# A fused RWKV-6 and GELU kernel: the last blocks' burst moved into the kv burst, the chunks' products in one burst by bank parity, and new slots

## The chip, the cores and the metric

The kernel runs on one core of a Trainium2 chip. The metric is the time of one execution in device microseconds (us). Before the change three runs gave 581.32, 579.07 and 582.42 us, a median of 581.32. Engines are named PE (TensorE), DVE (VectorE), ACT (ScalarE), POOL (GpSimd) and SP (SyncE, which issues most DMAs here).

## The reference

An RWKV-6 recurrence over 4 x 8 heads, 768 steps and a head size of 48, and behind it, token by token, a two-layer network with an exact GELU (384 to 2048 to 384, 3072 tokens), all in fp32:

```python
for t in range(S):
    cur = np.einsum('bhd,bhe->bhde', u[None] * kt, vt)
    y[:, :, t] = np.einsum('bhd,bhde->bhe', rt, state + cur)
    state = wt[:, :, :, None] * state + np.einsum('bhd,bhe->bhde', kt, vt)
x = y.transpose(0, 2, 1, 3).reshape(B * S, H * D)
h = x @ w_in
g = 0.5 * h * (1.0 + erf(h / sqrt(2)))
out = g @ w_out
```

## The kernel before

The tokens are cut into eight pieces of 384. For each piece `attention(x, unit)` makes the recurrence's output and leaves it, transposed, in `xT`; `mlp(x)` (for the first piece `first_mlp`) turns `xT` into 384 rows of the result. Both are Python generators, and the strings in `PLAN`, one for each stage, say in which order their steps are emitted: in stage x "." is a step of the network for piece x-1 on PE, "s" the second part of the recurrence for piece x, "f" the first part of the one for piece x+1, "v", "g", "o" and "e" the network's merges, GELUs, sums and copies (DVE, ACT, POOL), "l" loads, "x" and "w" sums of blocks of x and of the weights. The order of emission is the order of each engine's queue. Nothing else schedules: an engine takes its instructions in that order and waits on semaphores where data or a buffer is not ready. From stage 2 on the network's products follow a scheme of fewer multiplications with block sums (lists `PRODUCTS`, `OUT_PRODUCTS`), so that a stage holds 160 big matmuls (128x128 weights, 192 columns); an fp32 matmul shows as two records in the trace. Between them stand bursts of small 64x64 matmuls, which use the four quarters of the array.

The recurrence works in chunks of 64 steps. Inside a chunk it needs a lower triangle of products of r and k, scaled by running products of w, in `a_sb` (`at`). For pieces 2 to 7 `quarters()` builds it on two levels (`h` = 4 and 16). On each level twelve blocks (`n_b`) go through PE in three bursts (`cuts = (0, 5, 10, n_b)`: five, five and two blocks; 40, 40 and 16 records), each into a pair of PSUM banks of its own from `pair("d")`. From stage 2 on there are two such pairs, shared with `kv_ps` and `y_ps`. `copy_quarters` moves a burst's blocks into `at`: on the first level DVE with masks (L737), on the last ACT in six copies (`copy_rows`, L724). Between the bursts and the copies DVE scales r and k for the next level; on the last level k is then transposed in 32x32 blocks (L657), moved by 12 DMAs (L652) and four ACT copies (L806) to k transposed.

Then come, with `yield` between them:

- the burst `kv_ps` (L822): k transposed times v for each chunk, 96 records in two pairs of banks;
- `chain_states` (L837, L842): 20 small updates on DVE that carry the state from chunk to chunk, reading `kv_ps`;
- `inside()` (L863): the chunks' own products, `at` times v, 96 records into two pairs `y_ps`. For p = 0 and 1 the lower and the upper 64 rows of the array write to the pair's first and second bank;
- `fences()` (L873, L875): DVE copies two columns of `y_ps` to a tile that nobody reads, so that the states' products wait until the own products of both row halves are written;
- the products of r with the states (L908), 80 or 96 records, added into `y_ps`;
- the copies of `y_ps` to `xT` on ACT (L934, L931) and by DMA (L938).

Of the network, L1040 is `multiply`, L1084 and L1082 are ACT's copies out of PSUM, L1133 the GELU, L1115, L1117 and L1120 merges, L1161, L1164 and L1167 the sums for the output, L1036 and L1034 the sums of x. L512 and L499 begin the next piece's recurrence on DVE.

Of the kernel before, what the change touches and what calls it, by code (L numbers as in the profile page):

```python
# [38 lines left out]
PLAN = {  # L39
    0: "l.s....llsl.lssslslss.lc.l.slslls...ssss..lcs.s.s.l.ss..ss..sccs.c.s.llpssslw..cs.ffpccxx",  # L40
    1: (
        "l.ccswccclss.cw.l.ccccccscs.c.csscccc.scc.sscwccc.cswcs.wcsccscccls.c.ssc.sclcswcwcc.wcwcc"
        "sslcw..cwlclwccswclsc.cf.w.cw..ccc.cfw..cfyx....f.x..x.f.yxxf.wxw..y..y...wywyx..xyxf.yw.f"
        ".wxywxyl.yf."
    ),
    2: (
        "s.w..s.w.w.s..w..wswv.w..v.ww.vwv.ssw.swgww.swgsvwv.w.sgwv.wssls..wvsw...wg...g...wvsw.gvl"
        "s..sgvss...gg.ssvgvw.wvgvgvv.glsgv..gs.og.l.oe.s.wsoeo.s...seooe..l.so.ooe.lewo...o..ooeoe"
        "..os.eolol.s.se..oo.oew.lsw.ooosles..f.fo.oo.o.fo..xooxxfxxxxxfxfxx"
    ),  # L50
    3: (
        ".ls....v..s.sl...g...s.vvs..s..l.vg.gvg....s..l..sv.svss.ssss.g.svssgvlvg.sg..vv.vv.gsv.gv"
        "s.sggv.gslsvs..g.ogsog.e..s.eoo.....seo.oe.os.eoo.e...oooso.e.e.s.soo.ool.lessseo..oeolssf"
        "....fooo.e..f.xooxo.o..x.oooxlxxxfxfxfxx"
    ),
    4: (
        "ls.....s.ss.v....g....vlv.s.gs.vv..g....sv...s.glssvvgsvslsss..gvs.v.gs.ggss..v.sgv.vv..vv"
        ".slsggs.svsg.gog.g.s.oss.eo.e.o..o.so..ee..ooo..eoe.o..oosee.s..loo.os.oes.e.so.llsleo.of."
        "s.o.esolo.f..f.ooo.o.foo..xoxxxxxxxffxfxx"
    ),  # L60
    5: (
        ".....sll....v....vv..vsg.vs....ggs.v..vs.ls..g.sv.ssssvs.sl..g.vs.vsvgs.s.ggv.gss..l..vsvv"
        "vsssvg...ggsggogsg.os.oe.se.l.o..o..o.oe.es.o.oeeo....o..ooseoes..ose.loos.ssell..oo.eossf"
        "..o..fo.oeof..o..xoo.oxox.oxxlxxxffxfxx"
    ),
    6: (
        "s..sl...v.....v..g..ss.v.lvv...g.gvs..gsv..s.v..s.ssggsssvss..ss.l.vg.s..vg.vvggss..vvvv.."
        "ssssvggg..g.so.ggsoe...seo...ssols.o.o.eooe...o.e.eo.o.o.e.ooeo..ssl.oos.lsel..eslooo..lef"
        "s..oes.o.lfo..foo.o.o..fooxoxxxxxffxxxfxx"
    ),  # L70
    7: (
        "....sv.......gss.v....vsv..g..sg..vvg..s...s.svsgvsvss.ss.ss.vvgs.v.gsg.vg..svg...vv.ssgsv"
        "v.gg.g.sgso.gseo..es.....osso..ooo.eeoo..e.eso...oooee...os.soe..oos.se.s.oeosos...oo.e..."
        "oooo..oxo.oxx.oxxxxxxxx"
    ),
    8: (
        "..........v...v...v.v..g.gggv.v.....vv.....g.gvg....vgv.vvvgvgv..vgg..g.vgo..gge..eo...o.o"
        ".oo.eoe....oeo.e.o..o.oeeo..oo.eo.o.eo....ooe..o.e.oo.o..o.oo.oo.o"
    ),
}  # L80

# [111 lines left out]
def kernel(  # L193
# [31 lines left out]
    def pair(name):  # L225
        return pools["d"].tile([128, 2, BANK], F32, name=name, tag="d")
# [250 lines left out]
    def attention(x, unit):  # L477
# [183 lines left out]
        def quarters():  # L661
# [28 lines left out]
            for h in QUARTERS:  # L690
                m, r4, t4, s0, s1, s2 = views(h)

                def burst(first, behind):

                    d = pair("d")
                    if behind == n_b and h == FINE:
                        for a in range(FINE):
                            for g in range(2):
                                for p in range(2):
                                    nc.tensor.matmul(fine_of(d, g)[half[p], a * n_b:],  # L700
                                                     lhsT=places[half[g], a, p * C:(p + 1) * C],
                                                     rhs=fine_sb[half[g], 0:FINE - a, a],
                                                     start=(a == 0), stop=True, skip_group_check=True)
                    for n in range(first, behind):
                        i = n - first
                        for g in range(2):
                            for p in range(2):
                                nc.tensor.matmul(d[half[p], g, i * 3 * C // 2:(i + 1) * 3 * C // 2],  # L708
                                                 lhsT=kc[half[g], n // NI, n % NI, p],
                                                 rhs=rx[half[g], 2 * n + p], start=True, stop=True,  # L710
                                                 skip_group_check=True)
                    return d
# [99 lines left out]
        def vs(b, i, g):  # L812
            o = ((parts[b] * NI + i) * 2 + g) * D
            return loaded[x][1][:, o:o + G]

        kvs = []
        for b in range(np_):
            kv_ps = pair("kv_ps")
            for i in range(NI):
                for p in range(2):  # L820
                    for g in range(2):
                        nc.tensor.matmul(kv_ps[half[g], p, i * D:(i + 1) * D], lhsT=k_t(b, i, p, g),  # L822
                                         rhs=vs(b, i, g)[half[p], 0:D], start=True, stop=True)
# [21 lines left out]
        def swap(b):  # L845
            return parts[b] % 2
# [20 lines left out]
        def fences():  # L867

            for y, y_ps in ys:
                fence = wk.tile([128, 2], F32, name="fence")  # L870
                if split:
                    for c in range(2):
                        nc.vector.tensor_copy(out=fence[:, c:c + 1], in_=y[c][:, NI * C - 1:NI * C])  # L873
                else:
                    nc.vector.tensor_copy(out=fence, in_=y_ps[:, :, NI * C - 1])  # L875

        if x == 0:

# [18 lines left out]

        for i in range(NI):
            for p in range(2):
                for b in range(np_):  # L900
                    q, c3 = divmod(i, N3)
                    for g in range(2):
                        c = 2 * c3 + (p + g) % 2
                        src, c0 = (st, c - 1) if c else (before, NC - 1)
                        if src is None:
                            continue
                        o = ((parts[b] * Q + q) * NC + c0) * D
                        nc.tensor.matmul(ys[b][0][c % 2][half[g ^ swap(b)], i * C:(i + 1) * C],  # L908
                                         lhsT=src[half[g], o:o + G], rhs=rc[half[g], b, i, c % 2],
                                         start=False, stop=True, skip_group_check=True)  # L910
# [415 lines left out]
```

## Time and profile before

| what | value |
|---|---|
| runs, median (lowest to highest) | 581.32 us (579.07 to 582.42) |
| the profiled execution's own time | 584.98 us |
| its span from first to last instruction | 583.20 us |
| PE busy | 557.0 us, 96%, clock granted 1.0 |
| DVE busy | 491.9 us, 84% |
| ACT busy | 330.3 us, 57% |
| POOL busy | 103.1 us, 18% |
| DMA | 62.15 MB, mean 107 GB/s |

By stage (start and end in us, then busy us):

| stage | from | to | PE | DVE | ACT |
|---|---|---|---|---|---|
| 0 | 0 | 45.3 | 35.3 | 36.2 | 18.8 |
| 1 | 45.3 | 125.4 | 78.2 | 73.9 | 54.2 |
| 2 | 125.4 | 190.8 | 64.3 | 59.6 | 39.2 |
| 3 | 190.8 | 257.5 | 65.7 | 60.3 | 38.7 |
| 4 | 257.5 | 326.0 | 66.8 | 61.9 | 38.8 |
| 5 | 326.0 | 393.4 | 65.3 | 59.4 | 38.6 |
| 6 | 393.4 | 460.1 | 64.9 | 60.1 | 38.7 |
| 7 | 460.1 | 528.6 | 65.3 | 54.7 | 38.7 |
| 8 | 528.6 | 583.2 | 51.1 | 25.9 | 24.7 |

A timeline line has the start, the length, the engine, the line of the kernel, the operation, out<-in, the shape, how many were merged, and in brackets the idle time of the engine before it with what ended it. "issue" there means that the engine waited for nothing that the profile shows. A group's line ends with busy time, mean time of one, and idle time before them.

### The profile page before, as it was taken

How to read it: one execution, taken by the hardware profiler on the slowest of the kernel's cores; microseconds unless marked ns; L12 is line 12 of the kernel's file. 1: busy time of each engine (PE TensorE's matmuls, PEld its weight loads, DVE VectorE, ACT ScalarE, POOL GpSimd, SP SyncE). 2: the span in 40 equal slices, each digit the busy share in tenths (PEclk: the TensorE clock that was granted, in tenths of full speed). 3: DMA queues.
4: the chain of work that ended last, by engine and by line, in shares of the span. 5: the costliest groups of instructions: out<-in, count | busy, mean ns of one | idle time of the engine just before them, and what ended most of it. 6: DMA issues, size and time to landing. Idle time of an engine off the chain costs nothing. (4 is left out here: it accounts for less than half of the span.)

```text
span 583.2 us, 17698 instructions
## 1 busy us (share of the span) xinstructions
PE 557.0 (96%) x7410; PEld 492.4 (84%) x7424; DVE 491.9 (84%) x997; ACT 330.3 (57%) x733; POOL 103.1 (18%) x99
## 2 busy tenths in 40 slices
PE   6889999999999999999999999999999999999997
PEld 3675666579998988998898998999998988989997
DVE  6988979998989989799988988799888988855464
ACT  2368998027852575537763566527772568525820
POOL 3200000005400370005400352005500172000000
PEclk9999999999999999999999999999999999999999
DMA  7749850038633692337822693328814493201001
GB/s 244 214 127 365 305 204 12 28 111 115 80 77 104 148 160 31 90 97 151 116 37 80 177 141 43 79 75 174 111 27 126 108 118 47 41 14 42 0 1 40
DMA packets 71646, 62.15 MB, mean 107 GB/s; under 512 B 32912, under 2 KB 56720, under 8 KB 71568
## 3 DMA queue, kind: packets, MB, share of 16 engines
q1 hardware_dynamic: 50256, 45.62, 25.6%
q0 software_dynamic: 21216, 15.34, 20.0%
q8 instruction: 58, 0.95, 0.7%
q14 instruction: 20, 0.16, 0.1%
q10 hardware_dynamic: 96, 0.07, 0.1%
HBM read 36.24 MB, written 4.72 MB: 70 GB/s over the span
## 5 line engine op out<-in xcount | busy, mean ns | idle before, releaser
L1115 POOL DMA_DIRECT2D g<-o_sb x78 | 95.1, 1504 | 373.5 <-ACT g L1084 273.0
L1164 DVE TENSOR_TENSOR g<-g 128x512 f32<-128x512 f32 x112 | 75.1, 687 | 20.4 <-PE o_ps L1040 17.2
L1040 PE MATMUL h_ps<-forms_x,w_in_sb 128*128 128x192 f32 x280 | 58.2, 333 | 1.2 <-ACT g L1084 0.7
L1084 ACT COPY o_sb<-u_ps 128x384 f32<-128x384 f32 (+1 forms) x56 | 25.6, 458 | 54.0 <-PE u_ps L1040 52.5
L1040 PEld LDWEIGHTS h_ps<-forms_x,w_in_sb 128*128 128x128 f32 x280 | 46.2, 190 | 5.0 <-ACT g L1084 2.9
L1040 PE MATMUL o_ps<-w_out_sb,g 128*128 128x192 f32 x280 | 50.2, 326 | 0.0
L1084 ACT COPY g<-h_ps 128x384 f32<-128x384 f32 x84 | 40.1, 479 | 16.0 <-PE h_ps L1040 13.9
L1133 ACT ACTIVATE g<-g 128x384 f32<-128x384 f32 x98 | 46.4, 519 | 3.7 <-DMA g<-o_sb 2.6
L1040 PEld LDWEIGHTS o_ps<-w_out_sb,g 128*128 128x128 f32 x280 | 46.2, 190 | 0.3 <-ACT g L1133 0.3
L1040 PE MATMUL o_ps<-t,g 128*128 128x192 f32 x224 | 41.5, 328 | 0.2 <-DVE g L1120 0.2
L724 ACT COPY a_sb<-d 32x320 f32<-32x320 f32 (+5 forms) x108 | 39.1, 362 | 4.1 <-PE h_ps L1040 1.5
L1040 PEld LDWEIGHTS o_ps<-t,g 128*128 128x128 f32 x224 | 36.7, 190 | 1.1 <-DVE g L1120 0.5
L1040 PE MATMUL h_ps<-forms_x,s 128*128 128x192 f32 x168 | 35.9, 336 | 0.5 <-ACT u_ps L1084 0.3
L1051 PE MATMUL h_ps<-xT,w_in_sb 128*128 128x384 f32 x96 | 34.0, 497 | 1.2 <-ACT g L1053 1.0
L1040 PE MATMUL h_ps<-xT,w_in_sb 128*128 128x192 f32 x168 | 34.8, 330 | 0.0
L708 PE MATMUL d<-kx,rkw 64*64 64x96 f32 x1152 | 31.6, 248 | 2.5 <-ACT a_sb L724 1.5
L708 PEld LDWEIGHTS d<-kx,rkw 64*64 64x64 f32 x1152 | 25.5, 133 | 8.9 <-issue 3.8
L1040 PE MATMUL u_ps<-xT,w_in_sb 128*128 128x192 f32 x168 | 32.1, 327 | 0.1
L1040 PE MATMUL u_ps<-w_out_sb,g 128*128 128x192 f32 x168 | 31.3, 333 | 0.5 <-ACT u_ps L1084 0.5
L1059 PE MATMUL o_ps<-w_out_sb,g 128*128 128x384 f32 x96 | 31.4, 488 | 0.0
L573 PEld LDWEIGHTS d<-rkw 64*64 64x64 f32 x1152 | 20.3, 141 | 13.1 <-issue 7.1
L1040 PEld LDWEIGHTS h_ps<-forms_x,s 128*128 128x128 f32 x168 | 27.5, 189 | 4.1 <-ACT u_ps L1084 3.6
(169 smaller groups left out, 1199.3 us busy)
## 6 DMA issues: line engine op xcount, KB each, us to landing
g<-o_sb POOLq DMA_DIRECT2D x78, 192.0 KB, 4.2
rkw<-in_rkw_dram SPq DMA_DIRECT2D x54, 256.0 KB, 4.4
raw<-in_w_out_dram SPq DMA_DIRECT2D x8, 768.0 KB, 5.1
v_in<-in_v_dram SPq DMA_DIRECT2D x8, 584.0 KB, 4.0
out_dram<-o_sb SPq DMA_DIRECT2D x24, 192.0 KB, 1.9
raw<-in_w_in_dram SPq DMA_DIRECT2D x5, 768.0 KB, 10.3
rkw<-kx SPq DMA_DIRECT2D x72, 48.0 KB, 2.0
rkw<-in_rkw_dram SPq DMA_DIRECT2D x6, 384.0 KB, 6.6
```

Source lines behind the costliest of these rows:

```text
L573: nc.tensor.matmul(d[half[p], g, n * width:(n + 1) * width], lhsT=kc[half[g], b, i, p], rhs=right(half[g], b, i, p), start=True, stop=True)
L708: nc.tensor.matmul(d[half[p], g, i * 3 * C // 2:(i + 1) * 3 * C // 2], lhsT=kc[half[g], n // NI, n % NI, p], rhs=rx[half[g], 2 * n + p], s ...
L724: nc.scalar.copy(out=at[z, g, first:behind, (a + 1) * h:], in_=d[z, :, :, to] if g == slice(None) else d[z, :, to])
L1040: nc.tensor.matmul(o, lhsT=lhsT, rhs=rhs, start=start, stop=True, skip_group_check=True)
L1051: nc.tensor.matmul(h_ps, lhsT=w_in_sb[:, f // FI, j, f % FI * 128:(f % FI + 1) * 128], rhs=xT[:, j, :], start=(j == 0), stop=(j == NJ - 1))
L1059: nc.tensor.matmul(o, lhsT=gs[f // FG][:, f % FG, i * 128:(i + 1) * 128], rhs=w_out_sb[:, f, :], start=(f == 0), stop=(f == NF - 1))
L1084: nc.scalar.copy(out=o, in_=z)
L1115: nc.gpsimd.dma_start(out=o, in_=saved[q, t], accum_op=ALU.add)
L1133: nc.scalar.activation(out=o, in_=z, func=AF.Gelu, scale=MINUS.get(h, 1.0))
L1164: nc.vector.tensor_add(o, o, g_block(what[3:5]))
```

## The change

It does four things.

1. On the last level of `quarters()` the third burst (blocks 10 and 11) is no longer issued there. ACT copies the two blocks of k (256 columns) to a tile `kept` before DVE scales k; the burst is issued later, at the head of the kv burst, into the columns that kv leaves free in its first pair of banks, and its six copies into `at` follow on ACT right after the kv burst.
2. For pieces 1 to 7 the own products run by bank parity: in turn 0 one bank of each of the two pairs is written, in turn 1 the other. The products with the states follow in the same two turns. Their order changes too: the two row halves of neighbouring matmuls now go to one bank, before to two.
3. The fences of these pieces are made by ACT, two one-column copies ahead of each turn's states; before DVE made one copy of two columns for each pair.
4. All strings of `PLAN` but the first are new, so all engines' queues and SP's DMAs are interleaved anew in stages 1 to 8.

In the built order the small bursts of stages 2 to 7 fall from 39 to 32.

```diff
 PLAN = {
...
     7: (
-        "....sv.......gss.v....vsv..g..sg..vvg..s...s.svsgvsvss.ss.ss.vvgs.v.gsg.vg..svg...vv.ssgsv"
...
+        "........sss....v.vsgvs..s...vvg..gvv....s...s.vgvssvssgs.....sg..sg.vvss.ggss.svsgsvvgv.g."
...
-                def burst(first, behind):
+                def burst(first, behind, d=None, kn=None):
 
-                    d = pair("d")
+                    d = pair("d") if d is None else d
...
-                                                 lhsT=kc[half[g], n // NI, n % NI, p],
+                                                 lhsT=kn(half[g], n, p) if kn else kc[half[g], n // NI, n % NI, p],
...
-                ds.append(burst(*parts_of[2]))
+                if last:
+
+                    a, b = parts_of[2]
+                    kept = wk.tile([128, T], F32, name="ysb", bufs=1)
+                    nc.scalar.copy(out=kept[:, 0:(b - a) * 128], in_=k[:, a * 128:b * 128])
+
+                    def left(d, a=a, b=b, burst=burst, copy_quarters=copy_quarters, kept=kept):
+                        d = d[:, :, NI * D:]
+                        burst(a, b, d, lambda z, n, p: kept[z, (n - a) * 128 + p * C:(n - a) * 128 + (p + 1) * C])
+                        return lambda: copy_quarters(a, b, d)
+
+                    late.append(left)
+                else:
+                    ds.append(burst(*parts_of[2]))
...
-        last_r = []
+        last_r, late = [], []
...
             kv_ps = pair("kv_ps")
+            if b == 0:
+                late = [z(kv_ps) for z in late]
...
+        for z in late:
+            z()
         yield
...
-                fence = wk.tile([128, 2], F32, name="fence")
+                fence = wk.tile([128, 2 * NPART], F32, name="fence")[:, 0:2]
...
+        def states(order):
+            for i, b, c, g in order:
+                src, c0 = (st, c - 1) if c else (before, NC - 1)
+                if src is None:
+                    continue
+                o = ((parts[b] * Q + i // N3) * NC + c0) * D
+                nc.tensor.matmul(ys[b][0][c % 2][half[g ^ swap(b)], i * C:(i + 1) * C],
+                                 lhsT=src[half[g], o:o + G], rhs=rc[half[g], b, i, c % 2],
+                                 start=False, stop=True, skip_group_check=True)
+
...
             fences()
             yield
+            states((i, 0, 2 * (i % N3) + (p + g) % 2, g) for i in range(NI) for p in range(2) for g in range(2))
         else:
...
-            inside()
-            fences()
-            yield
-
-        for i in range(NI):
-            for p in range(2):
+            for _ in range(np_):
+                y_ps = pair("y_ps")
+                ys.append(([y_ps[:, c] for c in range(2)], y_ps))
+            for turn in range(2):
+                for i in range(NI):
+                    for b in range(np_):
+                        p = (b + turn) % 2
+                        for g in range(2):
+                            nc.tensor.matmul(ys[b][0][p][half[g ^ swap(b)], i * C:(i + 1) * C], lhsT=vs(b, i, g)[half[p]],
+                                             rhs=at[half[p], g, b * NI + i, :], start=(i == 0), stop=True, skip_group_check=True)
+            yield
+            fence = wk.tile([128, 2 * NPART], F32, name="fence")
+            for turn in range(2):
                 for b in range(np_):
-                    q, c3 = divmod(i, N3)
-                    for g in range(2):
-                        c = 2 * c3 + (p + g) % 2
...
+                    nc.scalar.copy(out=fence[:, turn * np_ + b:turn * np_ + b + 1], in_=ys[b][0][(b + turn) % 2][:, NI * C - 1:NI * C])
+                states((i, b, 2 * (i % N3) + (b + turn) % 2, g) for i in range(NI) for b in range(np_) for g in range(2))
```

More of the change, by code (lines that the diff above doesn't have):

```diff
@@ L71 @@
[L71 to L78 removed]
+        "wlcs.c.ccscsc.csccsc.c.wlsclsccclcscs.cwwlccc.scccss.scscccs.cscl.cssc.csc.ccl.scccwlwww.c"
@@ new lines @@
+        ".cs.ccl...cwc.fwcc.wcssfwf.fcw.fwc..cc..cwc.cf.wc.xwwcx.x.yyyw.ywyfyxy.y..wwy...f..x...wxx"
+        "xx.f.lxy.xy."
+    ),
+    2: (
+        "wl.ws..s.v...wsw..w.s.w.w.l..sl.wv.wwsgss.gwwv.s.v.wsg..wvwswsws.w..g.wvwvvv...vs..ssss.ws"
+        "swv..g.ggvsgwv.sw.gsgg.v.lgvvvv.gsg.w.goog.e..wwso..e..oos.o.oe.eo...lso.eo.ew.os.ooe.ess."
+        "lool..esloo..lffse.s..oolo.f.oe..w.oefo.o..ox.o.xsoox.oxxxoxxfxfwxx"
+    ),
+    3: (
+        ".....vsll.s.....v.s..s..vsg.gvs...vgs..v.v.sssv..sss.....sssgvg..gg.sv.ggs..vvgsss.s.s.svv"
+        "vvvsgvl.ggg.gs.g.eo.os..e.....soooe.o.oe.oo.o.o.eolle.s...loeoe.s.oosloe.s..lssel.oo.soefs"
+        "f....oo.eoo.f.o.o..olxoxo.xoxxfsxxxfxfxfxf"
+    ),
@@ new lines @@
+    4: (
+        "s...ll...v..s.....s..gs..vvg...vv.vg.vvg.l.s...s.ssvsgss...s.s.gsgsv..gssg.vgs..v.ssvsvvlg"
+        ".gvv..gvsgsg.og..oses.eo.sl...ooo...o.lseooe..e..ooe...eoe.o.o.sseoool..sles...so.esloso.o"
+        "..ff.feooof..oo..sooloxx..xoxxxxxfxfxfx"
+    ),
+    5: (
+        ".l...s....v.......gvs.v..sv.s.g.sg..vs...sgv.ssvsvssss..ss.vvvgs.g.....gsg.svgvsssslg.g.vg"
+        ".vvvsgv...gsgogo.ss.e.l.oes..o..os.eleoo.o.o.l.ooe.e.o...olee.oo..ososls.e..sle.loe.ososfs"
+        "..f.ooo..foe.l.ofo.o.ox.o.oxxxxxfxxfxfxx"
+    ),
@@ new lines @@
+    6: (
+        "......s.ss....v.vvs.g....v..v.s.gg..sg.gvvl..s.vsssgss.vs.s.gv.ss.gl.v.g..g.sssvs..sssvvgg"
+        "lvv.gvvs..s.ggo.g.o.e.e..ss.o..osooo.l.ee..olooooees......oee.olo.oeso.l.e.ls..ss.oosleos."
+        "..fof.eolo..f.oo.oo.fo.xoosxxxxxxxfxfxx"
+    ),
+    7: (
+        "........sss....v.vsgvs..s...vvg..gvv....s...s.vgvssvssgs.....sg..sg.vvss.ggss.svsgsvvgv.g."
+        "svggs.v.gg..s..oeos.eso..o....ooosoee..os.oo.eooe...ee..oso..ooes.s.ses..osseo..oo..ose..."
+        "o.o..ox.ox.oooxoxxxxxxxx"
+    ),
```

27 lines of the change are left out of this document (2 added, 25 removed).

## The prediction

> **What bounds the kernel now.** Views in this order: the page, the windows by stage, the timeline of TensorE (PE), all engines around kv and y, the groups by form, and the built order of both programs with its waits. PE is busy for 96% of the span at a granted clock of 1.0, so I looked for what the other 4% and PE's changes of shape cost. A "record" is one PE pass; an fp32 matmul is two. Stage n is what `PLAN[n]` places. Stages 2 to 8 begin at 125.4, 190.8, 257.5, 326.0, 393.4, 460.1 and 528.6 us.
>
> Stage 4 as a window; columns: length, busy time (instructions) of PE, PEld, DVE, ACT, POOL, clock, DMA share, GB/s:
>
> ```profile
> 257.50:326.00 68.50, 66.77 (x830) 62.69 (x830) 61.92 (x128) 38.79 (x95) 15.81 (x13) 1.00 0.53 105
> ```
>
> DVE is full to 90% as well: a wait on PE can only be removed while DVE follows.
>
> PE alone (start, length, what):
>
> ```profile
> 136.19 1.88 PE L708 MATMUL d<-kx,rkw 64*64 64x96 f32 x80
> 138.00 0.92 PE L1040 MATMUL h_ps<-forms_x,w_in_sb 128*128 128x192 f32 x4
> ...
> 182.85 0.95 PE L908 MATMUL y_ps<-rkw,st 64*64 64x64 f32 x28
> 184.53 1.03 PE L908 MATMUL y_ps<-rkw,st 64*64 64x64 f32 x52 [0.73 <-issue]
> ```
> ```profile
> 210.35 1.06 PE L708 MATMUL d<-kx,rkw 64*64 64x96 f32 x40
> 211.33 0.92 PE L1040 MATMUL h_ps<-forms_x,w_in_sb 128*128 128x192 f32 x4
> 212.18 1.06 PE L708 MATMUL d<-kx,rkw 64*64 64x96 f32 x40
> ```
> A small burst has a price of its own: 80 records take 1.81 us in one piece (136.19 to 138.00), two bursts of 40 take 2 x 0.98; and four big records take 0.85 (211.33 to 212.18) where a running row of them takes 0.65 (8 in 1.30). A burst less is worth 0.15 + 0.20 = 0.35 us. The gap before 184.53 has no releaser: it is code fetch.
>
> ```profile
> q8 instruction: 58, 0.95, 0.7%
> ```
> 58 packets make 0.95 MB, 16 KB each; PE's 7410 + 7424 instructions are 256 to a packet. Counted along the built order, this gap and those at 35.4 and 517.7 us lie at the same place modulo 256.
>
> Around kv and y in stages 3, 4 and 5:
>
> ```profile
> 241.26 1.67 PE L822 MATMUL kv_ps<-v_in,rkw 64*64 64x48 f32 x96
> 242.27 0.44 DVE L837 SCALAR_TENSOR_TENSOR st<-st,tot_sb,kv_ps 128x48 f32<-128x48 f32 x2
> 242.97 3.24 DVE L837 SCALAR_TENSOR_TENSOR st<-st,tot_sb,kv_ps 128x48 f32<-128x48 f32 x18 [0.26 <-PE kv_ps L822]
> 246.01 1.63 PE L863 MATMUL y_ps<-a_sb,v_in 64*64 64x64 f32 x96 [0.28 <-DVE st L837]
> 247.47 2.07 PE L908 MATMUL y_ps<-rkw,st 64*64 64x64 f32 x96
> ```
> ```profile
> 314.14 3.03 DVE L512 SCALAR_TENSOR_TENSOR kx<-rkw,u_sb 128x384 f32<-128x384 f32 x4
> 316.99 0.22 DVE L875 COPY fence<-y_ps 128x2 f32<-128x2 f32 x2
> 317.25 1.41 PE L908 MATMUL y_ps<-rkw,st 64*64 64x64 f32 x80 [0.79 <-DVE fence L875]
> ```
> ```profile
> 354.60 2.59 ACT L724 COPY a_sb<-d 32x320 f32<-32x320 f32 x6 [0.16 <-DVE a_sb L782]
> 357.25 0.56 PE L708 MATMUL d<-kx,rkw 64*64 64x96 f32 x16 [0.39 <-ACT a_sb L724]
> ```
> y waits for DVE's 20 state updates (0.18 us each) to free the pair of banks; the fence waits behind DVE's L512; the third burst waits for ACT to free its pair.
>
> The copies to be moved (groups by form: count | busy, mean ns | idle), and ACT behind y in stage 7:
>
> ```profile
> L724 ACT COPY a_sb<-d 16x192 f32<-16x192 f32 x12 | 3.7, 308 | 0.4
> L724 ACT COPY a_sb<-d 32x128 f32<-32x128 f32 x12 | 3.1, 255 | 0.1
> L724 ACT COPY a_sb<-d 16x64 f32<-16x64 f32 x12 | 2.4, 204 | 0.1
> ```
> ```profile
> 519.13 0.48 ACT L934 COPY ysb<-y_ps 128x384 f32<-128x384 f32 x1 [4.05 <-PE y_ps L908]
> 519.50 2.90 ACT L931 COPY xT<-y_ps 48x384 f32<-48x384 f32 x6
> ...
> 522.79 1.41 PE L1040 MATMUL u_ps<-w_out_sb,g 128*128 128x192 f32 x7 [0.27 <-ACT u_ps L1084]
> ```
>
> **The change, part by part** (us, against the profiled execution of 584.98 and its span of 583.20).
>
> A. Fewer bursts. In the built order stages 2 to 7 have 39 small bursts before and 32 after: 7 x 0.35 = **-2.4**.
>
> B. The third burst of the last level (16 records) goes into kv's burst. Its wait for ACT in stages 4 to 7 goes: intervals of 623 to 634 ns, 4 x 0.6 = -2.4. But what was late was ACT, whose six copies stood behind DVE's L782 (first fence of stage 5), and in both orders five or six gelus for the first out products stand behind these copies; now the new copy of k (256 columns, 0.37 from ACT's 128x192 at 0.32 and 128x384 at 0.48) is there too, and PE comes 0.6 + 0.35 sooner. I take all of it as given back at the first o_ps products: **0** (-2.4 if ACT has slack there, +1.2 if also the copy of k and the shorter bursts show).
>
> C. Fences. Before, PE loses 0.63 (stage 1), 0.37, 0.33, 0.86, 0.38, 0.87, 0.38 to them: 3.8. After, ACT makes them; but in the built program the pair's banks are one tile: the first two fence copies wait for all 96 records of the own products, both turns, and the next two for the first turn's states. So there are two handoffs in a row where there was one. One costs, from stage 3: 0.34 with a DVE copy of 0.16, that is 0.18 of way; two ACT copies (bound below 0.16, DVE's; I take 0.20, the 16x64 form) 0.18 + 0.40 less 0.13 of matmuls beside them = 0.47. Seven stages x 2, less one that two big matmuls hide in stage 2: 13 x 0.47 = 6.1, so **+2.3** (0 to +3).
>
> D. Code fetch. Before: gaps of 0.95 and 0.99 in stages 2 and 7. After, four packets are nearly all small (122 to 125 of 128 records); such packets lasted 3.05 to 3.9 before. Their records last 2.5 to 3.1, and the fence handoffs of C lie in them, which leaves about 0.3: **-1.6** (-1.9 to +2). [...]
>
> E. kv to y. The six moved copies last 2 x (0.255 + 0.308 + 0.204) = 1.53. In the built program they wait for the last kv matmul of the pair whose banks they read, and DVE's first state update waits for the count that the sixth copy raises. By stage 3: DVE began 1.01 after kv's start and, after a pause for the second pair, finished 20 updates so that y began at 4.75 with a wait of 0.28. Now: 16 records first (0.36, by 22.6 ns each), first pair ready at 1.37, six copies to 2.92, DVE from 2.98, the 18th update at 6.22, y at 6.4, its second pair 0.36 later. PE gets there at 1.9 + 0.2 + the big records between at 0.1625: 28, 20, 24, 20, 24, 16 in stages 2 to 7. Two first-copies of 0.26 come on top in stages 2, 4, 6. Waits: 0.5, 1.3, 1.2, 1.3, 1.2, 1.9 = 7.4, less 0.35 before: **+7.0** (+2 if half the copies overlap the updates, +8 with L1161's 0.36 among them). DVE's queue stands still behind the waiting update: L1188 to L1194 for the next out rows and L512 of the next chunk.
>
> F. ACT behind y: a copy of 0.48 and six of 0.47 precede the u_ps copy that a later product needs. With 10 big matmuls (20 records) after y, PE waited 0.43 (stage 7) and 0.35 (5), with 12 it was 0.17 (3). In the new order it is 8 in stages 4 and 6 (0.40 + 2 x 0.325 = 1.05 each), 10 in 3 and 5 (0.4 each), 12 in 2 and 7 (0.2): 3.3 against 0.95, **+2.4** (0 to +3.5).
>
> G. The rest of the new slots: all waits between big matmuls in stages 2 to 8 make some 13 us before; 10 are not named above. Longer pauses of PE at y let ACT and DVE catch up: **-2** (-4 to +3). Stages 0 and 1 keep their bursts, stage 0 its slots; the weight loads and chunk loads are interleaved anew on SP's queue, whose stage 1 had DMA at 0.48: 0.
>
> Sum: -2.4 + 0 + 2.3 - 1.6 + 7.0 + 2.4 - 2 = **+5.7**, a span of 588.9. The median of the runs (581.32) lies 3.7 below the profiled execution's time; the same step from it gives **587.0**.
>
> **Rivals.**
> 1. Faster: the waits of E hide. One mechanism: the path from the last h products to kv is shorter now (no third burst on it), kv's burst comes before its k copies and moves are needed, and DVE, who would pause, has its other work done by then. For it: 6.6 us of DVE's stage 4 are idle. Against: kv stands in stages 3 to 7 right where ACT's L806 ends. It decides once the copies start 2 us sooner against y. Then E = 0, B = -2.4, C = +1, F = 0: -2.4 - 2.4 + 1 - 1.6 = -5.4, **575.9**.
> 2. No change: gain and loss cancel, E at its lower end (+2), F at 0: +5.7 - 5 - 2.4 = -1.7, **579.6**, with G at 0 **581.6**.
> 3. Fetch decides: the long bursts wait for packets in spite of the fences, 4 x (3.9 - 2.9) = +4 instead of +0.3: **591**.
> 4. Row tiles collide. The states now write, in neighbouring matmuls of two row halves, one bank (two column halves of it) where the old order always used two banks; no row shows this form. If the array took such pairs in turn, a record of 64 columns would last 27 ns (half of 64 x 162.5/192) instead of 16.8: 624 records x 10 ns = +6.4, **593**; all in turn **+23**. [...]
>
> **How the numbers follow.** Forecast 0.58 (its own range 582 to 592), rival 1 0.20, rival 2 0.10, rival 3 0.07, rival 4 0.05. About 0.5%, 2.9 us, can be told from no change here. Slower: 0.52 of the forecast + 0.07 + 0.05 = 0.64; same: 0.06 + 0.04 of rival 1 + 0.08 of rival 2 = 0.18; faster 0.16 + 0.02 = 0.18. The range 576 to 594 takes in rivals 1 to 4 but for the last one's far end.
>
> **What would show it.** A: 32 bursts. B: no wait at d, but waits for ACT's gelus at the first o_ps. C: two waits on ACT's fence in one y burst, some 0.45 each. D: no gap without releaser inside y. E: ACT's six copies from kv_ps, then DVE's first update, y waiting over 1 us for st. F: u_ps waits near 1 us in stages 4 and 6. Wrong if y begins with no wait in stages 3 to 7, or if a state record lasts well over 17 ns.

## The result and the profile after

| | us, median (lowest to highest) | profiled execution, its own time and span |
|---|---|---|
| before, 6 runs | 581.79 (579.07 to 582.45) | 584.98, 583.20 |
| changed, 6 runs | 599.91 (596.88 to 600.64) | 599.63, 597.9 |
| changed, once more on another chip, 6 runs beside 17 of before at 584.02 | 598.39 (597.45 to 600.91) | 598.02, 596.3 |

The change makes the kernel slower: ratio 1.031, 95% interval 1.028 to 1.034; on the second chip 1.0269 (1.0242 to 1.0296). By spans of the first two profiles it costs 14.7 us, by medians 18.1, on the second chip 14.4. 587.0 was forecast.

Length of the stages, from the first big matmul of each to that of the next:

| profile | 0 and 1 | 2 | 3 | 4 | 5 | 6 | 7 | 8 |
|---|---|---|---|---|---|---|---|---|
| before | 125.42 | 65.38 | 66.84 | 66.25 | 67.66 | 66.60 | 68.64 | 56.41 |
| before, again | 126.81 | 65.43 | 66.86 | 66.48 | 66.30 | 66.54 | 68.01 | 56.42 |
| changed | 129.35 | 67.30 | 67.65 | 70.79 | 68.73 | 67.91 | 69.70 | 56.42 |
| changed, again | 126.11 | 67.03 | 67.63 | 71.19 | 68.75 | 69.39 | 69.74 | 56.41 |

The loss is in every stage that has a recurrence beside the network (2 to 7), and most in stage 4. Stage 8, which has none, keeps its time to 0.02 us. (Counted this way stages 5 to 8 of the first profile before begin at 323.89, 391.55, 458.15 and 526.79 us, some 2 us earlier than in the table by stage above.)

Around kv and y in stage 3 of the changed kernel, all engines (start, length, engine, line, operation, out<-in, shape, count, idle time before it and what ended it):

```profile
245.43 0.56 PE L708 MATMUL kv_ps<-kx,ysb 64*64 64x96 f32 x16
...
245.81 2.01 PE L837 MATMUL kv_ps<-v_in,rkw 64*64 64x48 f32 x96
...
247.16 1.63 ACT L724 COPY a_sb<-kv_ps 32x128 f32<-32x128 f32 x6 [1.30 <-PE kv_ps L837]
...
247.75 1.57 PE L1067 MATMUL u_ps<-w_out_sb,g 128*128 128x192 f32 x8
...
248.82 3.59 DVE L854 SCALAR_TENSOR_TENSOR st<-st,tot_sb,kv_ps 128x48 f32<-128x48 f32 x20 [2.33 <-ACT a_sb L724]
...
252.21 0.88 PE L930 MATMUL y_ps<-a_sb,v_in 64*64 64x64 f32 x25 [0.81 <-DVE st L854]
```

(This view ends at 252.9, so it shows the first 25 of y's 96 records.) The 16 moved records and kv's 96 take from 245.43 to 247.75, 2.32 us. ACT's six copies end at 248.8, and only then DVE begins its 20 updates, after 2.33 us without work; y waits 0.81 for them. Before, DVE began 1.01 after kv's start, here 3.01 after the first of the 96. The updates' group on the page:

```profile
L854 DVE SCALAR_TENSOR_TENSOR st<-st,tot_sb,kv_ps 128x48 f32<-128x48 f32 x160 | 28.8, 258 | 7.0 <-ACT a_sb L724 6.9
```

The updates last as long as ever; the 6.9 us of idle time that ACT's copies end are new.

PE alone in stage 4, then PE and ACT behind y in stage 7:

```profile
322.08 1.96 PE L930 MATMUL y_ps<-a_sb,v_in 64*64 64x64 f32 x96 [0.70 <-DVE st L854]
324.38 0.73 PE L900 MATMUL y_ps<-rkw,st 64*64 64x64 f32 x29 [0.33 <-ACT fence L936]
325.80 0.45 PE L900 MATMUL y_ps<-rkw,st 64*64 64x64 f32 x11 [0.69 <-issue]
326.41 0.91 PE L900 MATMUL y_ps<-rkw,st 64*64 64x64 f32 x40 [0.17 <-ACT fence L936]
```
```profile
530.25 0.98 PE L900 MATMUL y_ps<-rkw,st 64*64 64x64 f32 x48 [0.27 <-ACT fence L936]
...
531.42 0.98 PE L900 MATMUL y_ps<-rkw,st 64*64 64x64 f32 x48 [0.20 <-ACT fence L936]
...
532.45 0.48 ACT L961 COPY ysb<-y_ps 128x384 f32<-128x384 f32 x1 [1.01 <-PE y_ps L900]
532.82 2.90 ACT L958 COPY xT<-y_ps 48x384 f32<-48x384 f32 x6
...
536.13 1.08 PE L1067 MATMUL u_ps<-w_out_sb,g 128*128 128x192 f32 x5 [0.94 <-ACT o_sb L1109]
```

Two waits for ACT's fence stand in every y but that of stage 2, which has one, and in stage 4 a gap that nothing in the profile releases (0.69 of idle time, 0.91 from start to start), as those that were read as code fetch before (what supports that reading stands in the last section). Behind y PE waits 0.94 for a product that ACT copies only after its seven copies of `y_ps`.

What PE lost in stages 2 to 7, summed from the starts of its records: each interval less the running rate of its kind (162.5 ns between big records, 16.1 between small ones), sorted by what ended it. Two profiles of each kernel:

| lost by PE, us | before | again | changed | again | mean change |
|---|---|---|---|---|---|
| changes between big and small records | 8.26 | 8.50 | 6.74 | 6.74 | -1.6 |
| wait for the state updates ahead of y | 0.44 | 0.44 | 5.34 | 5.35 | +4.9 |
| fences | 3.23 | 2.26 | 4.78 | 4.82 | +2.1 |
| ACT's copies of u_ps and o_sb, most of them behind y | 2.39 | 2.79 | 5.27 | 5.02 | +2.6 |
| gaps without releaser among like records | 3.50 | 3.87 | 3.90 | 4.90 | +0.7 |
| small records slower than 16.1 ns | 4.06 | 3.98 | 6.38 | 6.52 | +2.4 |
| waits at the bursts d and at kv | 5.95 | 4.74 | 4.29 | 4.64 | -0.9 |
| other waits of the output's products | 3.55 | 2.88 | 4.78 | 5.22 | +1.8 |
| big records slower than 162.5 ns | 9.30 | 9.49 | 9.90 | 9.83 | +0.5 |
| sum | 40.68 | 38.95 | 51.40 | 53.05 | +12.4 |

Three rows need a closer look. The gaps without releaser are of two kinds. Those of 0.6 us and more are 0.93 and 0.98 before (0.99, 1.12 and 0.70 in the second profile), 0.89 changed (0.87 and 1.24): 0.9 less in the mean. But five gaps of 0.22 inside y, one in each of stages 3 to 7, are new: each of these records starts 0.15 after a state update of DVE ends, so they belong to the wait for the updates, 1.1 more. Of ACT's copies, 0.95 is lost behind y before (0.91 again), and 4.64 after (4.39 again), 3.6 more; the other waits of that row fell by 1.0. And of the small records' loss, 1.5 is in kv's own records and 1.0 in those of y.

### The profile page after: what moved, and what is told of

It reads as the page before. It is cut to its first block, busy times and chain, and to the rows that moved or that the text cites. A ratio compares the mean times of both kernels' runs of the same rounds, so it can differ in the third digit from the quotient of the medians.

```text
span 597.9 us, 17706 instructions
## 1 busy us (share of the span) xinstructions
PE 565.1 (95%) x7424; PEld 498.2 (83%) x7424; DVE 490.7 (82%) x983; ACT 336.0 (56%) x767; POOL 103.0 (17%) x99
## 4 chain that ended last, share of the span: by engine, by line
PE 65%; ACT 13%; DVE 11%; issue 5%; DMA 3%; SPq 1%; ACTq 1%; POOL 1%; DVEq 0%; POOLq 0%
PE u_ps L1067 17%; PE o_ps L1067 13%; PE h_ps L1067 13%; PE o_ps L1086 5%; ACT a_sb L724 3%; DVE st L854 3%; PE d L573 3%; PE h_ps L1078 3%; PE d L708 3%; PE y_ps L900 3%; ACT xT L958 2%; PE y_ps L930 2%; DMA g<-o_sb 1%; PE kv_ps L837 1%; DMA rkw<-in_rkw_dram 1%
## 5 line engine op out<-in xcount | busy, mean ns | idle before, releaser
L854 DVE SCALAR_TENSOR_TENSOR st<-st,tot_sb,kv_ps 128x48 f32<-128x48 f32 x160 | 28.8, 258 | 7.0 <-ACT a_sb L724 6.9
L1078 PE MATMUL h_ps<-xT,w_in_sb 128*128 128x384 f32 x96 | 34.0, 506 | 0.4 <-ACT g L1080 0.4
L1067 PEld LDWEIGHTS u_ps<-w_out_sb,g 128*128 128x128 f32 x168 | 27.1, 190 | 6.6 <-ACT u_ps L1111 3.6
L724 ACT COPY a_sb<-d 32x320 f32<-32x320 f32 (+2 forms) x72 | 29.9, 416 | 2.4 <-PE d L708 1.1
L573 PEld LDWEIGHTS d<-rkw 64*64 64x64 f32 x1152 | 19.8, 140 | 13.7 <-issue 7.7
```

The costliest lines, as they stand in the source:

```text
L573: nc.tensor.matmul(d[half[p], g, n * width:(n + 1) * width], lhsT=kc[half[g], b, i, p], rhs=right(half[g], b, i, p), start=True, stop=True)
L724: nc.scalar.copy(out=at[z, g, first:behind, (a + 1) * h:], in_=d[z, :, :, to] if g == slice(None) else d[z, :, to])
L854: nc.vector.scalar_tensor_tensor(out=stq[:, q, c], in0=stq[:, q, c - 1] if c else b4[:, q, NC - 1], scalar=totq[:, q, c:c + 1], in1=kvs[q ...
L1067: nc.tensor.matmul(o, lhsT=lhsT, rhs=rhs, start=start, stop=True, skip_group_check=True)
L1078: nc.tensor.matmul(h_ps, lhsT=w_in_sb[:, f // FI, j, f % FI * 128:(f % FI + 1) * 128], rhs=xT[:, j, :], start=(j == 0), stop=(j == NJ - 1))
```

## The experiments

All ratios are to the kernel before, run on the same chip in the same minutes, with 95% intervals.

### Code and slots exchanged

The strings of `PLAN` fit both codes but for one step: the new code needs one step fewer in each piece. The first three runs did not allow for that.

**e1_code_old_slots**: the new code, every string of `PLAN` the old one.

```diff
 PLAN = {
...
-        "wl.ws..s.v...wsw..w.s.w.w.l..sl.wv.wwsgss.gwwv.s.v.wsg..wvwswsws.w..g.wvwvvv...vs..ssss.ws"
+        "s.w..s.w.w.s..w..wswv.w..v.ww.vwv.ssw.swgww.swgsvwv.w.sgwv.wssls..wvsw...wg...g...wvsw.gvl"
...
```

> The new code (late burst, parity, ACT fences) with the old slots of all stages. Theory 'code': most of the 18 us sits in the waits of the code itself (y behind the six late ACT copies 7.7, fences 5.9 against 3.8, a longer kv burst 2.6, less 2.4 for seven bursts fewer), so 590 to 596 us, with DVE's first state update behind the ACT copies as in the changed kernel. Theory 'slots': the new order of stages 1 to 8 loses it, so this stays within 2 us of before plus 5, 583 to 588 us. The matmuls at half clock in stages 0 and 1 should be gone in both.

Measured: 626.94 us, ratio 1.0724 (1.0669 to 1.078). **e2_new_slots_old_code**, the same exchange the other way, and **e4_no_late**, the changed kernel with its last burst back in place (`if last:` made `if False:` in `quarters()`):

> The old code with the new slots of stages 1 to 8. Theory 'code': stages 0 and 1 lose up to 4 us by the new slots of stage 1, the others about nothing, 583 to 587 us. Theory 'slots': 592 to 598 us. If the two parts add, this run's distance from before and that of the run with the new code in old slots sum to about 18 us; if they don't, new slots and new code only suit each other.

> The changed kernel with the last blocks' burst back in its own place (nothing late), new slots kept. Theory 'late copies': y's wait of 7.7 us and 2.6 us of the longer kv burst go, six bursts of their own come back at 0.35 each, so -8 us, 590 to 593 us, and DVE's first state update waits for PE again. Rival 'cover': the time that y waited is only handed on to the next handoff (u_ps, the GELUs), so 597 to 600 us.

Measured: 654.44 us (1.1199, 1.1136 to 1.1262) and 652.05 us (1.1175, 1.1109 to 1.1242). In e1 all steps behind the second burst's copies come one slot early; in e2 and e4 one slot late, and there the sums of x read `xT` before its last copies (in e4's stage 2 the first two sums run at 196.49 and 197.02 us, ACT's copies to `xT` from 200.62 on). So none of the three tells code from slots. What they do show is the price of a step that is one slot off its place: 22 to 53 us over the aligned versions that follow (e5, e6, e7).

**e5_code_old_slots_aligned** repeats e1 with an empty step where the old code had its third copies; **e6_new_slots_old_code_aligned** repeats e2, **e7_no_late_aligned** repeats e4, with second and third copies in one step; **e8_late_alone_old_slots** is e5 with the old `inside()`, `fences()` and order of the states.

```diff
                 for z, d in list(zip(parts_of, ds))[1:]:
                     copy_quarters(*z, d)
-                    yield
+                    if not last or z[1] == n_b:
+                        yield
```

(e6 and e7; e5 and e8 keep the `yield` and add `if last: yield` behind the loop.)

> New code in the old slots, with an empty step where the old code copied its third burst, so that every later step of the recurrence falls where it fell in the kernel before (without it, the steps behind came one slot early and the time was 627 us). Theory 'code': late copies ahead of y, fences and the longer kv burst cost about as in the changed kernel, 592 to 596 us. Theory 'slots': the code costs little in slots that fit it, 583 to 587 us.

> Old code in the new slots, the second and third burst's copies of the last level in one step so that the later steps fall into the changed kernel's slots. Theory 'code': stages 0 and 1 cost up to 4 us, the rest nothing, 583 to 588 us. Theory 'slots': 592 to 598 us. If code and slots add, this run's and the previous run's distances from before sum to 16 to 19 us.

> The changed kernel with the last blocks' burst in its own place again (their copies in the second copies' step, later steps in the same slots). Theory 'late copies': the waits ahead of y (7.7 us) and the excess of the kv burst (2.6) go, six bursts come back (6 x 0.35 = 2.1), so 8 us less than the changed kernel, 590 to 594 us, and DVE's first state update waits for PE instead of ACT. Rival 'cover': the freed time turns up in the next handoffs, 597 to 600 us.

> Of the code's changes the late burst alone, in the old slots (an empty step for the third copies). Theory 'late copies': y waits for the state updates behind six ACT copies, about 7.7, kv burst 2.6, seven bursts... six fewer 2.1: 8 us over before, 589 to 593 us on a chip where before takes 582. Rival: in the old slots the copies are covered, 580 to 584 us.

| ratio | old slots | new slots |
|---|---|---|
| old code | 1 | e6: 1.0371 (1.0338 to 1.0405) |
| late burst alone | e8: 1.0227 (1.0195 to 1.0258) | |
| parity and ACT fences alone | | e7: 1.0242 (1.0206 to 1.0279) |
| all of the new code | e5: 1.0341 (1.0281 to 1.0401) | 1.031 and 1.0269 |

Medians were 604.59 (e5), 605.45 (e6), 598.92 (e7) and 597.18 (e8), with before at 584.52. Code alone costs 20 us, slots alone 21, both together 14 to 18: they don't add, so both theories as they were put fall. The late burst by itself costs 13 us in the old slots, more than the 8 that were expected; what parity and fences add there, another 7, is partly stage 1. In e5 stage 1 reads (all engines, start, length and so on as above):

```profile
89.51 1.63 PE L932 MATMUL y_ps<-a_sb,v_in 64*64 64x64 f32 x96
...
91.51 1.00 ACT L458 ACTIVATE e<-raw,two 128x768 f32<-128x768 uint32 x1
...
92.54 1.07 ACT L460 ACTIVATE e<-raw 128x768 f16<-128x768 f32 x1
...
93.48 0.20 ACT L938 COPY fence<-y_ps 128x1 f32<-128x1 f32 x2
...
93.68 0.96 PE L902 MATMUL y_ps<-rkw,st 64*64 64x64 f32 x48 [2.55 <-ACT fence L938]
```

The own products end at 91.1, but ACT converts weights until 93.5; PE stands still for 2.55 us. In the changed kernel's own slots for stage 1 PE stands still for 0.27 and 0.20 us at the two fences. In e7 PE no longer waits for the state updates (0.44 us in all, 5.34 in the changed kernel), but the waits for ACT behind y and at the bursts d and kv grow from 9.6 to 18.2 us: the theory "cover" was nearer (expected 597 to 600, measured 598.9). With the old code the same two rows are 19.8. So these slots leave ACT late when the third burst and its copies stand in their old place. That it is the long wait ahead of y that lets ACT catch up in the changed kernel is not shown: e9 below has neither that wait nor these, but its ACT has the six copies less to make.

### Stage 1

**e3_old_slots_stage1**: the changed kernel with the old string for stage 1. **e13_stage1_old**: that, and the old own products and DVE fences for the piece of stage 1 (`if x == 1:` around the old lines). **e14_changed_again**: no edit.

```diff
 PLAN = {
...
     1: (
-        "wlcs.c.ccscsc.csccsc.c.wlsclsccclcscs.cwwlccc.scccss.scscccs.cscl.cssc.csc.ccl.scccwlwww.c"
+        "l.ccswccclss.cw.l.ccccccscs.c.csscccc.scc.sscwccc.cswcs.wcsccscccls.c.ssc.sclcswcwcc.wcwcc"
...
```

> The changed kernel with the old string for stage 1 alone. Theory 'idle then half clock': the new order of stage 1 puts the first level's burst ahead of the first network matmuls, PE idles 1.9 us behind ACT and the granted clock falls to one half for two times 3.4 us; with the old string both are gone and the run is 3.5 to 4.5 us shorter, 595 to 596.5 us. Rival 'code position': the longer fetch gap at 37 us comes from where the instructions fall in the packets, not from stage 1's order; then at least the first half-clock stretch stays and the run is 598 to 600 us.

> The changed kernel with stage 1 as it was: its old slots together with its old own products and DVE fences. Theory 'stage 1 fits only itself': the profiles with the new slots of stage 1 reach stage 2 at 126.1 to 129.4 us, those with old slots and new fences at 129.0 and 130.7, those with both old at 125.4 and 125.5; so here 125.5 again, no matmuls at half clock between 30 and 125 us, and 2.5 to 4 us under the changed kernel. Rival 'chance': the spread of stages 0 and 1 comes from transfers and not from what is in stage 1; no difference from the changed kernel.

> The changed kernel once more, beside the others on one chip: ratio 1.028 to 1.034. If the half clock in stages 0 and 1 is not chance, it shows again where PE stood still for more than half of a window of 3.4 us.

Measured: e3 599.56 us (1.0281, 1.0232 to 1.033), e13 600.19 (1.0289, 1.0259 to 1.0319), e14 598.39 (1.0269, 1.0242 to 1.0296). No version of stage 1 moves the time, and the profile of the changed kernel taken again reaches stage 2 at 126.11 us, not 129.35; e13's, with all of stage 1 old, at 130.11. "Chance" holds. PE in the changed kernel, first and second profile, at the same instructions:

```profile
34.53 0.91 PE L837 MATMUL kv_ps<-v_in,kx 64*64 64x48 f32 x46
37.23 0.20 PE L837 MATMUL kv_ps<-v_in,kx 64*64 64x48 f32 x1 [1.79 <-issue]
...
38.34 3.44 PE L900 MATMUL y_ps<-rkw,st 64*64 64x64 f32 x78
```
```profile
34.52 0.91 PE L837 MATMUL kv_ps<-v_in,kx 64*64 64x48 f32 x46
36.67 0.20 PE L837 MATMUL kv_ps<-v_in,kx 64*64 64x48 f32 x1 [1.24 <-issue]
...
37.43 1.33 PE L900 MATMUL y_ps<-rkw,st 64*64 64x64 f32 x40
39.29 1.38 PE L900 MATMUL y_ps<-rkw,st 64*64 64x64 f32 x38 [0.52 <-DVE fence L890]
```

The same gap, at one and the same record, lasts 1.79 us in one execution and 1.24 in the other. After the longer one 78 records take 3.44 us, which in the other take 1.33 and 1.38: the clock granted to PE from 37.6 to 41.0 us was 0.50 (see the last section). From start to start it is 2.00 and 1.46 us; before's two profiles have 1.02 and 1.73.

### The late copies

**e9_late_copies_left_out**, **e10_late_copies_twice** and **e17_late_copies_after_updates**:

```diff
-        for z in late:
-            z()
         yield
```
```diff
-        for z in late:
+        for z in late * 2:
             z()
```
```diff
-        for z in late:
-            z()
         yield
...
                 chain_states(range(c, min(c + 2, NC - 1 + int(first))))
+                if c == 4:
+                    for z in late:
+                        z()
```

> The changed kernel without the six ACT copies of the last two blocks (their part of the chunks' own products keeps old numbers). Theory 'late copies on the path': the waits for the state updates ahead of y (5.3 us in stages 2 to 7, and 0.24 x 5 inside y) go, 4.5 to 6.5 us less than the changed kernel, ratio 1.020 to 1.024. Rival 'cover': DVE has no other slack and y waits for its 20 updates all the same, less than 2 us.

> The changed kernel with the six copies made twice. Theory 'late copies on the path': 1.53 us more in each of six stages ahead of DVE's first update, all of it seen by y, 9 us over the changed kernel, ratio about 1.046. Rival 'cover': less than 3 us.

> The changed kernel with the six late copies issued behind the state updates instead of ahead of them; in the built order ACT's copies now wait for DVE's last update that reads their banks. Theory 'in a row': copies and updates read the same pair of banks one after the other in either order, so y starts as late as before, ratio 1.024 to 1.031; y's wait is now for ACT's copies. Rival 'DVE's queue': what cost was DVE standing still behind its first update, 1.5 us of its queue in each stage; then 3 to 6 us less, ratio 1.017 to 1.022.

Measured: e9 591.12 us (1.0137, 1.0091 to 1.0182), e10 609.71 (1.0455, 1.0411 to 1.0499), e17 598.51 (1.0265, 1.0227 to 1.0303). "On the path" holds on both sides. Without the copies stages 2 to 7 are 6.6 us shorter than in the first profile of the changed kernel, and PE's wait for the updates is 0.44 us as before the change. Twice the copies cost 9 us more than once, 6 x 1.53 as counted. In e9 the view of the updates' line says who is waited for now:

```profile
  PE kv_ps L837: 2.7, 6
```

(Idle time of DVE ahead of the updates, and how often: PE again, and nothing of ACT.) By the ratio e9 is 8 to 10 us under the changed kernel, more than the 4.5 to 6.5 expected; the stages of its profile account for 6.6 of it against the first profile of the changed kernel and 8.2 against the second. In e10 most of the price does not show at y: the waits for the updates are 2.0 longer (7.29 us), and PE waits 5.0 more for ACT's copies of the output's products a little ahead of y, which stand behind the doubled copies in ACT's queue. So the copies cost twice over, by the updates that wait for their banks and by what waits behind them on ACT. e17 turns the order round. Stage 3 of e17, all engines:

```profile
243.37 0.44 DVE L852 SCALAR_TENSOR_TENSOR st<-st,tot_sb,kv_ps 128x48 f32<-128x48 f32 x2 [0.67 <-PE kv_ps L837]
244.07 3.24 DVE L852 SCALAR_TENSOR_TENSOR st<-st,tot_sb,kv_ps 128x48 f32<-128x48 f32 x18 [0.26 <-PE kv_ps L837]
247.05 1.64 ACT L724 COPY a_sb<-kv_ps 32x128 f32<-32x128 f32 x6 [3.99 <-DVE st L852]
248.71 0.32 ACT L1112 COPY o_sb<-u_ps 128x192 f32<-128x192 f32 x1
...
249.08 0.92 PE L1068 MATMUL u_ps<-t,g 128*128 128x192 f32 x4 [2.25 <-ACT o_sb L1112]
249.93 1.63 PE L931 MATMUL y_ps<-a_sb,v_in 64*64 64x64 f32 x96
```

DVE starts at once, but now ACT stands still 3.99 us until the last update has read the banks, and behind its six copies is one that PE needs: PE waits 2.25 us a little ahead of y instead of 0.81 at y. In stages 4 and 6 y itself waits for these copies (4.0 us together). Copies and updates are one chain in either order, because they read the same banks and the built program lets one engine in after the other; no run here lets both read them at once. The rival (DVE's queue standing still) falls.

### The fences

**e11_one_fence_round**: two ACT copies of two columns, then the states of both turns. **e12_one_fence_round_dve**: the same by DVE. **e15_stage1_old_one_round**: e11 and e13 together. **e16_before_act_fences**: the kernel before, ACT instead of DVE for the fences of stages 2 to 7.

```diff
+            for b in range(np_):
+                nc.scalar.copy(out=fence[:, 2 * b:2 * b + 2], in_=ys[b][1][:, :, NI * C - 1])
             for turn in range(2):
-                for b in range(np_):
-                    nc.scalar.copy(out=fence[:, turn * np_ + b:turn * np_ + b + 1], in_=ys[b][0][(b + turn) % 2][:, NI * C - 1:NI * C])
```
```diff
-                    nc.vector.tensor_copy(out=fence, in_=y_ps[:, :, NI * C - 1])
+                    (nc.scalar.copy if x > 1 else nc.vector.tensor_copy)(out=fence, in_=y_ps[:, :, NI * C - 1])
```

> The changed kernel with one round of ACT fences (two copies of two columns, then the states of both turns) where it has two. Theory 'two handoffs in a row': seven times 0.4 less, 2.8 us under the changed kernel, ratio 1.026. Rival: ACT reaches its copies of y sooner and nothing else moves, so the u_ps waits take it back, no difference.

> The same single round made by DVE. Theory: DVE's fence waits 0.35 where its queue is free and 0.9 or more where it stands behind the next piece's first operations (L512), so about the cost of the single ACT round or up to 2 us more; if ACT in stage 1 is what costs there, stage 1 gets shorter by some 0.3.

> Stage 1 as it was and one round of ACT fences from stage 2 on. If the terms add: 3 us from stage 1 and 2.3 us of fence handoffs off the changed kernel, ratio 1.020 to 1.023; what is left over the kernel before is then the late copies (6.6 us) and the other waits of the new slots. Rival 'fetch takes it back': the longer row of records without a pause waits 0.9 to 1.5 us for code inside y in stages 4 and 6, ratio 1.026.

> The kernel before with ACT in place of DVE for the fences of stages 2 to 7, nothing else. If DVE's queue is what makes two of its fences long (0.95 us at the head of the burst in stages 4 and 6), up to 1.2 us less; ACT's copies cost 0.47 a stage where DVE's cost 0.35, 0.4 us more. Together 0.5 to 1 us less, not told from no change, ratio 0.997 to 1.001.

Measured: e11 596.46 us (1.0222, 1.0191 to 1.0253), e12 608.24 (1.0421, 1.0387 to 1.0455), e15 595.82 (1.0224, 1.0192 to 1.0256), e16 583.97 (1.0000, 0.9975 to 1.0025). One round halves the fences' waits, 4.78 to 2.47 us in stages 2 to 7, as expected; the median fell a little more, by 3 to 5 us depending on which run of the changed kernel it is held against. In the profile the gaps without releaser took it back, 3.90 to 6.92; stage 6 of e11, PE alone:

```profile
456.08 1.97 PE L930 MATMUL y_ps<-a_sb,v_in 64*64 64x64 f32 x96 [0.63 <-DVE st L854]
458.37 0.68 PE L900 MATMUL y_ps<-rkw,st 64*64 64x64 f32 x23 [0.33 <-ACT fence L935]
460.36 1.83 PE L900 MATMUL y_ps<-rkw,st 64*64 64x64 f32 x57 [1.31 <-issue]
```

One engine changed (e12) costs 12 us against e11, far more than the 2 expected. In stage 2 of e12:

```profile
189.15 0.19 DVE L935 COPY fence<-y_ps 128x2 f32<-128x2 f32 x2
...
189.39 2.47 PE L900 MATMUL y_ps<-rkw,st 64*64 64x64 f32 x80 [3.14 <-DVE fence L935]
```

PE stands still for 3.14 us there and 2.36 in stage 3: in the new slots DVE's fence stands behind its work for the next piece (in stage 2, 3.01 us of L512 and 1.78 of L499). In the old slots (e16) it makes no difference which engine does it. e15 is e11 over again, so stage 1 adds nothing. None of the versions beats the kernel before.

**e18_before_again**, no edit:

> The kernel before once more, with a profile: how far stages differ between two profiles of one kernel. If the fetch gaps and the half clock of stage 0 come and go by chance, stage 2 begins somewhere from 123 to 127 us, and stages 2 to 7 differ by up to 1 us each.

Measured: 584.75 us (1.0014, 0.9982 to 1.0045). Stage 2 begins at 126.81; stages 2 to 7 are the same to 0.25 us but for 5 (1.36 less) and 7 (0.63 less).

## Why the prediction was wrong, step by step

Slower was right, by its largest term; the size was short: +5.7 on the span was forecast, 14.7 was profiled. For stages 2 to 7 the terms made 5.4 and the mean of two profiles each is +12.4. The missing 7 us, term by term:

- **A**, fewer bursts, failed, and was the largest miss. There are 32 bursts, and changes of kind cost 1.6 less, not 2.4. But the moved burst saved nothing inside kv: 16 and 96 records take 2.32 us together, as they did apart (0.56 and 1.67), so kv's own records lose 1.5 more than before. A is -0.2, not -2.4.
- **B** was nearly right in its sum: ACT's waits at the third burst (2.45 us) are gone, and the rest of that row and the output's products lost 3.4 in their place, so +0.9 for 0, inside its bounds. The place was half right, and the rest luck: 1.0 of it stands at ACT's gelus and copies for the o_ps products, as was said, 1.3 at bursts that wait for DVE's scaled k, and 1.0 inside kv of stage 4, behind the DMAs of k transposed.
- **C** was right: +2.1 in stages 2 to 7, and in stage 1 the fences cost 0.90 where they cost 0.63, forecast 2.3 in all; e11 confirms that the second round is half of it.
- **D** was mis-sized: -0.9 for -1.6. The gaps inside y of stages 2 and 7 went, but stage 4 has one in both profiles (0.91 from start to start in the first), and stage 6 in the second profile of either kernel. The fences' pauses were counted as cover that leaves 0.3; in stage 4 a gap stands between the two fences all the same. Where such a gap falls and how long it lasts varies from run to run.
- **E** was right in mechanism and nearly in size: +4.9 ahead of y and 1.1 inside it, 6.0 for 7.0. Stage by stage it is none, 1.2, 1.1, 1.2, 1.0 and 2.0 in stages 2 to 7, forecast 0.5, 1.3, 1.2, 1.3, 1.2 and 1.9. e9 and e10 show it to be on the path, e17 why.
- **F** was right in mechanism and short in size, +3.6 for 2.4. Stages 3 to 6 lost 0.42, 1.13, 0.42 and 1.11 behind y, forecast 0.4, 1.05, 0.4 and 1.05; but stage 7 lost 1.10 where 0.2 was forecast, because the product that waits there comes after 8 big matmuls, not after 12.
- **G** failed: "Longer pauses of PE at y let ACT and DVE catch up: -2". What is left for it is about -0.5: 1.0 less of waits for ACT's copies elsewhere, and big records at a slower pace, +0.5. The step named a gain without a row that priced it, and took no account of what the new slots lose by themselves: with the late burst back in its old place (e7) the two rows of ACT's copies and of the bursts d and kv make 18.2 us, against 9.6 in the changed kernel and 8.3 before.
- **No term** stood for y's own records, which lose 1.0 more, nor for the shorter gaps, 0.5 more. What makes both longer stays open.
- **Stages 0 and 1**, put at 0, took 3.9 us in the first profile. e14 and e18 show that two profiles of one kernel differ by 3.2 and 1.4 there, and e13, with all of stage 1 old, is no shorter; no part of the change was found behind it.

The step from the span to the median hid another 3 us: the first profile of before was 3.2 above its runs' median and the changed kernel's was not.

**Rivals.** 1 (the waits of E hide) is refuted by e9 and e10. 2 likewise. 3 (fetch decides) is refuted for the changed kernel, whose gaps of 0.6 us and more are 0.9 less than before; in e11's profile the two inside y of stages 4 and 6 are 2.7 together. 4 (row halves collide in one bank) is refuted: a record of the states starts 17.1 ns after the one ahead of it on average in the changed kernel, 16.0 before, where it needed 27.

## What to carry to other kernels

Work that is moved into another burst is not free when the readers of those banks come one after the other: here one engine's 1.5 us of copies went in series with another's updates, six times (in stage 3 DVE stood 2.33 us without work until they ended), and doubling or leaving out the copies shows in one run each that they are on the path, and exchanging the order of the two engines shows that they are in series. Slots and code that were planned for each other are one change; either alone cost as much as both, so a part's price is read only with the schedule that belongs to it, and a step one slot off costs more than the change itself. A gain that is to come from one engine's longer pauses should be priced by the waits that it would end, row by row, and not by the idle time that the pauses make.

## What the runs showed of the hardware

PE's granted clock. In the changed kernel's first profile it is 0.50 for 3.41 us from 37.56 us and from 47.80 us, and from 597.34 us to the end; behind the first 14 us it is 1.00 otherwise. The second and third of these starts lie 3 and 164 steps of 3.413 us behind the first, on one grid through the whole execution. All three come right behind windows in which PE did little (0.42 us of 3.41 ahead of the third). That profile by such windows (length, busy time and instructions of PE, PEld, DVE, ACT, POOL, clock, DMA share, GB/s):

```profile
34.20:37.60 3.40, 1.61 (x103) 1.45 (x95) 2.00 (x13) 3.04 (x4) 0.00 (x0) 0.99 0.50 175
37.60:41.00 3.40, 3.40 (x99) 3.40 (x91) 2.15 (x13) 0.27 (x1) 0.00 (x0) 0.50 0.02 5
41.00:44.40 3.40, 3.40 (x130) 2.72 (x126) 3.07 (x5) 0.20 (x1) 0.00 (x0) 1.00 0.13 27
44.40:47.80 3.40, 1.48 (x58) 1.03 (x60) 3.19 (x11) 2.77 (x6) 0.00 (x0) 1.00 0.73 242
47.80:51.30 3.50, 3.50 (x52) 2.48 (x50) 2.69 (x4) 3.09 (x4) 0.00 (x0) 0.51 0.97 309
```

PE is busy 1.61 and 1.48 of 3.4 us (47% and 44%), and the window behind each has a clock of 0.50 and 0.51. Over all 20 profiles of this study, without the first 12 us: of windows with PE busy under 40%, 28 of 28 were followed by half clock; between 40 and 50%, 12 of 23; above, 17 of 3384. So waits well short of a window can cost more than themselves where they fall into one window: here they were the gap of 1.79 us ahead of 37.23 us and 1.92 us behind ACT ahead of 46.65, and in e5 2.55 us behind ACT's fence (PE busy 1.00 us of 3.40) were followed by a window at 0.51.

Code fetch. All 20 profiles, without the first 12 us, hold 80 gaps of 0.65 us and more between like records of PE that no semaphore ends. Each of the 80 ends 1.25 to 1.59 us after one of its profile's instruction packets of 16 KB has landed (in the changed kernel's first profile those at 37.23 and 325.80 us 1.30 and 1.38 us after), which is why they are read as PE waiting for code. Such a gap is not a constant: the same record of stage 0 was late by 1.0 to 2.3 us from start to start in different executions, and of the seven profiles in which it was 2.0 us or more, five had the next window at half clock. Of the 3.2 us by which the two profiles of the changed kernel reach stage 2 apart, 2.88 stand already at the first record of L1078 (49.07 and 46.19 us), behind this gap and, in the first, the window at half clock.
